# A replanned prologue order in a sliding-window attention and SwiGLU kernel

## The chip, the cores and the metric

The kernel runs on one core of a Trainium2 chip. The time is that of the device, in microseconds (us), from one launch; the kernel before has a median of 340.18 us over 11 runs (338.02 to 342.67). The engines of the core run side by side, each with its own list of instructions in order: PE (TensorE, matmuls), ACT (ScalarE), DVE (VectorE), POOL (GpSimd) and SP (SyncE). Here POOL issues the loads from memory, and SP issues copies and transposes by DMA.

## What is computed

The reference is causal attention with a window of 64 keys, and a SwiGLU layer on its output:

```python
# q, k, v: (8, 8, 576, 64) = batch, heads, positions, head size; float32
scores = q @ k.T / 8                                  # per batch and head
mask = (rel >= 0) & (rel < 64)                        # rel = query - key position
attn = softmax(where(mask, scores, -1e9))
x = (attn @ v) with heads side by side                # (4608, 512)
g = x @ w_gate                                        # (4608, 1536)
out = (g * sigmoid(g) * (x @ w_val)) @ w_out          # (4608, 512), float32
```

## The kernel before

The 4608 tokens (8 batches one behind the other) are cut into 36 chunks of 128 tokens for the attention, and into 9 groups of 512 tokens, four chunks each, for the SwiGLU layer. The 1536 hidden features are 12 blocks of 128. All matmuls are in bf16, and the loads cast on the way.

A chunk `n` goes through these steps, each a method of `_Kernel`; in the plan's entries the letter stands first and the chunk behind it:

- `ld` (`load`, line 328): POOL issues the DMA of q, k or v of the chunk into a ring of buffers, 4 for q, 4 for k (chunk modulo 4) and 10 for v. A load waits until the buffer's last reader is done. A third number is a gate: the load waits for the scores `S` of that chunk. Chunks 4, 13 and others that cross a batch's end come in two DMAs. The first two chunks of q and k are different: `first_loads` brings them as float32 by SP and ACT into the space of hT1, and `first_cast` casts them.
- `Tpe` (line 495): PE transposes q or k of a chunk, four 128x128 blocks into one PSUM bank, and ACT or DVE copies it into qT or kT. `T` (line 384) does the same as one DMA transpose on SP's queue.
- `shift` (line 347): the v tokens of a chunk are copied to a second layout, vb, offset by 64 tokens, since each half chunk of 64 queries looks at 128 keys. ACT, DVE or SP does it.
- `S` (line 400): 16 matmuls of q and k, two exps on ACT, and the mask: either a product with 0 or 1 on DVE, or (the flag `True`) a bias of -30000 that two more 512-wide matmuls add in PSUM. It needs kT of the chunk and of the one before.
- `AV` (line 437): 16 matmuls of the exps with vb and va (a column of ones gives the sums), and on DVE a reciprocal and a product, into xb.
- `X` (line 463): xb is transposed into xT, by PE and a copy, or by a DMA transpose where the plan says `'sp'`.
- `F` (`c, f0, nf, u0, u1`, line 537): for group c, nf feature blocks from f0 and chunks u0 to u1 of the group: gate and value matmuls (four steps of 128 features each), tanh on ACT (`sig`), two DVE operations (`uu`, `hT`). A whole `F` is 512 columns wide, cut either as one block by four chunks, two by two, or four by one.
- `O` (line 559): the 12 matmuls with w_out for one chunk, a copy on ACT, and the store.
- `W` (line 369) and `load_wo` (line 375): loads of feature blocks of the gate weights ('g'), the value weights ('v') and w_out, also issued by POOL.
- `warm` (line 512): matmuls of 512 columns on zeros, whose result nobody reads. `init...`: constants, mostly memsets on DVE.

`build` (line 634) first runs through the list `PLAN` (lines 151 to 198), then through a fixed `period` for groups 2 to 8, twice per group. The list holds the prologue: all attention up to chunk 11, scores of 12 and 13, all of groups 0 and 1 as far as `F` is concerned, and the four `O` of group 0. The order of the list is the order in which every engine gets its own instructions; nothing reorders them later. `_Graph` (line 31) records what each operation reads and writes, and places semaphore waits where one engine needs another's result. Every DMA takes the next of 16 counters ("lanes") of its queue, and the 17th waits for the landing of the first.

PSUM has 8 banks. In the list before the first `F`, transposes, scores and AV take turns in seven of them; from the first `F` on, four belong to `F` and four to the rest; from the first `O` on, three to the rest and one to `O`.

Of the kernel before, what the change touches and what calls it, by code (L numbers as in the profile page):

```python
# [7 lines left out]
B, H, S, D = 8, 8, 576, 64  # L8
DM, DFF = H * D, 1536
T = B * S  # L10
# [138 lines left out]

class _Kernel:  # L150
    PLAN = [
        ('first_loads', 0), ('init_va', 3, 4), ('init_va', 0, 1), ('first_loads', 1), ('init_va', 5, 6),
        ('init_va', 1, 2), ('init_va', 2, 3), ('init_va', 7, 8), ('init',), ('init_pt', 1, 'act'),
        ('first_cast', 0, 'k', 'act'), ('init_kT',), ('init_pt', 3, 'act'), ('ld', 'k', 5), ('ld', 'q', 4),
        ('init_va', 8, 9), ('warm', 7), ('init_pt', 2, 'act'), ('ld', 'k', 2), ('init_mask',),
        ('Tpe', 0, 'k', 'dve'), ('warm', 5), ('ld', 'v', 1), ('warm', 1), ('ld', 'k', 3),
        ('first_cast', 1, 'q', 'act'), ('shift', 0, 1, 'dve'), ('Tpe', 1, 'q', 'dve'), ('warm', 2),
        ('shift', 0, 0, 'act'), ('Tpe', 5, 'k', 'dve'), ('first_cast', 1, 'k', 'act'), ('ld', 'q', 3), ('init_vb',),
        ('Tpe', 4, 'q', 'dve'), ('Tpe', 1, 'k', 'dve'), ('ld', 'q', 2), ('Tpe', 2, 'k', 'dve'),
        ('shift', 1, 0, 'dve'), ('first_cast', 0, 'q', 'act'), ('ld', 'v', 3), ('Tpe', 0, 'q', 'act'),  # L160
        ('ld', 'k', 4), ('init_pt', 0, 'dve'), ('ld', 'v', 2), ('S', 1, True, False), ('init_va', 4, 5),
        ('S', 0, True, False), ('shift', 1, 1, 'dve'), ('Tpe', 3, 'k', 'dve'), ('AV', 1), ('ld', 'k', 6),
        ('Tpe', 3, 'q', 'act'), ('ld', 'k', 7), ('AV', 0), ('ld', 'q', 7), ('Tpe', 2, 'q', 'dve'),
        ('shift', 3, 0, 'act'), ('ld', 'q', 6), ('X', 1, 'act'), ('ld', 'q', 5), ('S', 3, True, False),
        ('shift', 2, 1, 'dve'), ('ld', 'v', 4), ('shift', 2, 0, 'act'), ('Tpe', 4, 'k', 'dve'), ('X', 0, 'dve'),
        ('S', 2, True, False), ('AV', 3), ('Tpe', 6, 'k', 'dve'), ('W', 'v', 3, 4), ('S', 4, True, False), ('AV', 2),
        ('Tpe', 7, 'k', 'act'), ('Tpe', 6, 'q', 'dve'), ('Tpe', 7, 'q', 'dve'), ('W', 'g', 3, 4), ('X', 3, 'act'),
        ('W', 'g', 4, 6), ('shift', 4, 0, 'dve'), ('W', 'v', 4, 6), ('W', 'g', 10, 12), ('ld', 'v', 5),
        ('shift', 3, 1, 'act'), ('X', 2, 'dve'), ('Tpe', 5, 'q', 'dve'), ('S', 6, False, False), ('W', 'v', 10, 12),
        ('S', 7, True, False), ('AV', 4), ('W', 'g', 0, 3), ('W', 'v', 0, 3), ('F', 0, 3, 1, 0, 4), ('ld', 'q', 8),  # L170
        ('F', 0, 5, 1, 0, 4), ('F', 0, 4, 1, 0, 4), ('shift', 4, 1, 'act'), ('W', 'v', 6, 8), ('ld', 'v', 6),
        ('ld', 'k', 11), ('W', 'g', 6, 9), ('S', 5, False, False), ('F', 0, 10, 2, 2, 4), ('shift', 5, 0, 'act'),
        ('F', 0, 10, 2, 0, 2), ('X', 4, 'act'), ('ld', 'q', 9), ('AV', 5), ('shift', 5, 1, 'act'), ('W', 'v', 8, 10),
        ('ld', 'k', 10), ('init_va', 6, 7), ('F', 0, 0, 3, 1, 2), ('W', 'g', 9, 10), ('ld', 'v', 13, 7),
        ('ld', 'k', 9), ('ld', 'q', 10), ('F', 0, 1, 2, 2, 4), ('ld', 'v', 7), ('Tpe', 8, 'q', 'act'),
        ('shift', 13, 0, 'sp'), ('ld', 'k', 8), ('X', 5, 'act'), ('init_va', 9, 10), ('F', 0, 0, 3, 0, 1),
        ('T', 11, 'k'), ('F', 1, 0, 2, 0, 2), ('F', 1, 3, 4, 0, 1), ('F', 0, 6, 3, 2, 3), ('shift', 6, 0, 'act'),
        ('F', 0, 0, 1, 2, 4), ('ld', 'v', 8), ('Tpe', 10, 'k', 'act'), ('F', 0, 6, 3, 3, 4), ('ld', 'q', 11),
        ('F', 0, 6, 3, 1, 2), ('shift', 6, 1, 'act'), ('AV', 6), ('ld', 'v', 9), ('shift', 7, 0, 'act'),
        ('F', 1, 8, 4, 0, 1), ('Tpe', 9, 'q', 'act'), ('ld', 'v', 12, 6), ('F', 1, 7, 1, 0, 1), ('AV', 7),  # L180
        ('load_wo', 0, 6), ('X', 6, 'act'), ('Tpe', 10, 'q', 'act'), ('load_wo', 6, 12), ('ld', 'v', 10),
        ('T', 8, 'k'), ('F', 0, 6, 3, 0, 1), ('F', 0, 9, 1, 0, 4), ('Tpe', 11, 'q', 'act'), ('X', 7, 'dve'),
        ('Tpe', 9, 'k', 'act'), ('F', 1, 5, 2, 1, 3), ('ld', 'q', 13, 7), ('ld', 'k', 12, 7),
        ('S', 10, False, False), ('ld', 'v', 11), ('S', 8, False, False), ('F', 1, 0, 2, 2, 4),
        ('shift', 8, 1, 'dve'), ('T', 12, 'k'), ('shift', 8, 0, 'act'), ('shift', 12, 1, 'sp'), ('F', 1, 8, 4, 3, 4),
        ('shift', 9, 0, 'dve'), ('ld', 'q', 12, 7), ('shift', 7, 1, 'dve'), ('T', 13, 'q'), ('S', 9, False, False),
        ('shift', 9, 1, 'act'), ('S', 11, False, False), ('F', 1, 10, 2, 1, 3), ('O', 0, 3), ('shift', 10, 0, 'act'),
        ('AV', 8), ('shift', 11, 0, 'act'), ('shift', 10, 1, 'dve'), ('ld', 'k', 15, 11), ('F', 1, 5, 3, 3, 4),
        ('T', 15, 'k'), ('O', 0, 2), ('X', 8, 'sp'), ('AV', 9), ('ld', 'q', 15, 9), ('ld', 'k', 13, 8),
        ('F', 1, 8, 2, 1, 3), ('T', 13, 'k'), ('F', 1, 7, 1, 1, 3), ('AV', 11), ('O', 0, 1), ('T', 12, 'q'),  # L190
        ('AV', 10), ('F', 1, 3, 2, 1, 3), ('ld', 'q', 14, 9), ('S', 13, False, False), ('S', 12, False, True),
        ('X', 9, 'sp'), ('F', 1, 2, 1, 0, 4), ('F', 1, 3, 1, 3, 4), ('ld', 'k', 16, 12), ('ld', 'k', 14, 8),
        ('shift', 12, 0, 'sp'), ('ld', 'v', 14, 10), ('ld', 'k', 17, 11), ('X', 11, 'sp'), ('X', 10, 'sp'),
        ('T', 15, 'q'), ('T', 14, 'q'), ('T', 14, 'k'), ('ld', 'q', 16, 11), ('ld', 'v', 15, 9), ('ld', 'q', 17, 11),
        ('shift', 11, 1, 'dve'), ('shift', 14, 1, 'sp'), ('ld', 'v', 17, 12), ('O', 0, 0), ('shift', 14, 0, 'sp'),
        ('F', 1, 4, 1, 3, 4), ('shift', 15, 1, 'sp'), ('ld', 'v', 16, 10), ('shift', 13, 1, 'sp'),
        ('shift', 15, 0, 'sp'),
    ]

    NQ = 4  # L200
# [489 lines left out]
```

## Time and profile before

| | |
|---|---|
| median of 11 runs | 340.18 us |
| the profiled execution | 342.18 us |
| its span, first to last instruction | 340.4 us |
| PE busy in the span | 326.6 us (96%) |
| DVE, ACT, POOL busy | 220.5, 145.3, 108.4 us |
| first `F` on PE begins | 23.67 us |
| first `O` on PE begins | 68.58 us |
| first period begins (its first `F`) | 89.68 us |
| clock granted to PE, mean of the span | 0.995 |

The slice rows cut the span into 40 equal parts of 8.5 us; a digit is the busy share in tenths. In a row of waits stand the waiting engine and line, who ended the wait, the sum, the number and the longest. In a row of the timeline stand the start, the time to the end, engine, line, operation and count; the end of a matmul is modelled, so that a group overlaps the next by some 0.17 us, and what counts is the distance from start to start. In a row of stretches stand the limits, their length, the busy time of PE with the number of instructions, the granted clock, the busy share of the DMA engines and GB/s. In a row of DMA issues stand the count, the size of one, and the median time from issue to landing.

The DMA slices of the prologue are full:

```profile
DMA  9999999997999999979899969696973202101022
GB/s 161 155 161 188 181 163 155 141 157 158 158 155 138 191 173 111 175 114 173 114 173 113 168 105 173 113 169 134 149 131 80 62 33 62 40 24 63 0 91 97
```

### The profile page before, as it was taken

The page shows a single profiled execution, that of the slowest core. Times are in us where ns is not written, and L with a number is a line of the kernel's source. Part 1 is how long each engine was busy: PE and PEld are TensorE (multiplying, and loading weights), DVE is VectorE, ACT ScalarE, POOL GpSimd, SP SyncE. Part 2 cuts the span into 40 slices and gives each one's busy share as a digit, 9 for nine tenths or more (in the row PEclk, how much of TensorE's full clock was granted, in tenths as well). Part 3 has the DMA queues.
Part 4 walks back from the last instruction along what each step waited for, and adds up shares of the span by engine and source line. Part 5 has one row for each costly group of instructions (what it writes and reads, how often), then busy time and mean ns, then how long its engine had stood idle before and what let it go on. Part 6 is the DMA issues. An engine that isn't in the chain of part 4 may idle for free.

```text
span 340.4 us, 7150 instructions
## 1 busy us (share of the span) xinstructions
PE 326.6 (96%) x2869; PEld 181.2 (53%) x2903; DVE 220.5 (65%) x477; ACT 145.3 (43%) x258; POOL 108.4 (32%) x135
## 2 busy tenths in 40 slices
PE   6988998999999999999999999999999999999996
PEld 2665997767544445444444444545454545444444
DVE  4786888677793939393939393939394948283610
ACT  5885566553443425252525243434343433223221
POOL 8999911430841423423232325141400000000000
PEclk9999999799999999999999999999999999999999
DMA  9999999997999999979899969696973202101022
GB/s 161 155 161 188 181 163 155 141 157 158 158 155 138 191 173 111 175 114 173 114 173 113 168 105 173 113 169 134 149 131 80 62 33 62 40 24 63 0 91 97
DMA packets 171969, 43.39 MB, mean 127 GB/s; under 512 B 158048, under 2 KB 167456, under 8 KB 171936
## 3 DMA queue, kind: packets, MB, share of 16 engines
q0 software_dynamic: 116256, 18.36, 82.2%
q1 hardware_dynamic: 48416, 14.74, 27.2%
q10 hardware_dynamic: 7264, 9.83, 8.8%
q8 instruction: 23, 0.38, 0.5%
q14 instruction: 10, 0.08, 0.1%
HBM read 37.75 MB, written 9.44 MB: 139 GB/s over the span
## 4 chain that ended last, share of the span: by engine, by line
PE 56%; DVE 19%; DMA 9%; POOL 6%; ACT 4%; issue 3%; ACTq 1%
PE ps L569 27%; PE ps L530 26%; DVE uu L551 8%; DVE hT L553 6%; DMA kn<-in_k_dram 4%; DVE xb L460 3%; DMA kT<-kn 3%; ACT ost L574 2%; DMA hT<-in_q_dram 2%; ACT sig L546 2%; POOL qn L345 2%; POOL Wg L373 1%; POOL va L345 1%; DVE rc L457 1%; POOL Wv L373 1%
## 5 line engine op out<-in xcount | busy, mean ns | idle before, releaser
L551 DVE SCALAR_TENSOR_TENSOR uu<-sig,ps 128x512 bf16<-128x512 bf16 (+3 forms) x113 | 74.6, 660 | 87.3 <-ACT sig L546 86.0
L530 PE MATMUL ps<-xT,Wv 128*128 128x512 bf16 (+2 forms) x579 | 112.7, 327 | 0.4 <-DMA Wv<-in_moe_w_val_dram 0.3
L530 PE MATMUL ps<-xT,Wg 128*128 128x512 bf16 (+2 forms) x554 | 107.3, 324 | 4.2 <-DVE uu L551 1.4
L546 ACT ACTIVATE sig<-ps 128x512 bf16<-128x512 f32 (+3 forms) x113 | 65.6, 582 | 87.4 <-PE ps L530 86.7
L569 PE MATMUL ps<-Wo,hT 128*128 128x512 bf16 x413 | 95.0, 379 | 0.4
L553 DVE SCALAR_TENSOR_TENSOR hT<-uu,ps 128x512 bf16<-128x512 bf16 (+3 forms) x113 | 75.0, 663 | 4.4 <-PE ps L530 0.5
L530 PEld LDWEIGHTS ps<-xT,Wv 128*128 128x128 bf16 x580 | 51.6, 99 | 43.9 <-issue 0.8
L345 POOL DMA_DIRECT2D kn<-in_k_dram x38 | 33.3, 881 | 124.4 <-PE ps L420 116.6
L530 PEld LDWEIGHTS ps<-xT,Wg 128*128 128x128 bf16 x580 | 48.5, 99 | 36.8 <-issue 1.9
L569 PEld LDWEIGHTS ps<-Wo,hT 128*128 128x128 bf16 x420 | 41.0, 98 | 48.6
L574 ACT ACTIVATE ost<-ps 128x512 f32<-128x512 f32 x35 | 20.9, 597 | 84.5 <-PE ps L569 84.5
L433 ACT ACTIVATE pt<-ps 128x512 bf16<-128x512 f32 x72 | 37.5, 599 | 10.0 <-PE ps L420 10.0
L345 POOL DMA_DIRECT2D va<-in_v_dram x40 | 36.3, 927 | 0.8 <-POOLq L675 0.8
L345 POOL DMA_DIRECT2D qn<-in_q_dram x38 | 33.5, 888 | 8.1 <-PE ps L530 8.1
L460 DVE TENSOR_TENSOR xb<-ps,rc 128x256 bf16<-128x256 f32 x72 | 30.6, 425 | 2.5
L435 DVE TENSOR_TENSOR pt<-pt,mask 128x512 bf16<-128x512 bf16 x60 | 23.6, 422 | 2.8 <-ACT pt L433 1.7
L451 PE MATMUL ps<-va,pt 128*128 128x65 bf16 x288 | 22.5, 193 | 0.0
L450 PE MATMUL ps<-vb,pt 128*128 128x65 bf16 x288 | 22.4, 193 | 0.0
L450 PEld LDWEIGHTS ps<-vb,pt 128*128 128x128 bf16 x288 | 20.0, 98 | 3.5
L451 PEld LDWEIGHTS ps<-va,pt 128*128 128x128 bf16 x288 | 18.9, 97 | 3.2
L420 PEld LDWEIGHTS ps<-qT,kT 64*128 64x128 bf16 x576 | 9.8, 95 | 10.7 <-issue 7.8
L420 PE MATMUL ps<-qT,kT 64*128 64x64 bf16 x576 | 12.6, 191 | 2.3 <-DMA kT<-kn 1.8
(47 smaller groups left out, 101.5 us busy)
## 6 DMA issues: line engine op xcount, KB each, us to landing
out_dram<-ost ACTq DMA_DIRECT2D x35, 256.0 KB, 4.0
va<-in_v_dram POOLq DMA_DIRECT2D x32, 128.0 KB, 7.4
kn<-in_k_dram POOLq DMA_DIRECT2D x30, 128.0 KB, 5.7
qn<-in_q_dram POOLq DMA_DIRECT2D x30, 128.0 KB, 6.4
vb<-va SPq DMA_DIRECT2D x47, 80.0 KB, 4.5
Wo<-in_moe_w_out_dram POOLq DMA_DIRECT2D x2, 768.0 KB, 21.3
Wv<-in_moe_w_val_dram POOLq DMA_DIRECT2D x4, 256.0 KB, 9.9
Wg<-in_moe_w_gate_dram POOLq DMA_DIRECT2D x2, 384.0 KB, 11.0
```

The costliest lines, as they stand in the source:

```text
L345: self.g.op("pool", lambda e, d=d, a=a: e.dma_start(d, a), reads=gate, writes=ks, dma=True)
L433: g.op("act", lambda e, po=po, p=p: e.activation(po, sv[p], ACTF.Exp, scale=SCALE), reads=[bx[p][1]], writes=[pk])
L435: g.op("dve", lambda e, po=po: e.tensor_tensor(po, po, m, ALU.mult), reads=[pk, "mask"], writes=[pk])
L450: e.matmul(av[:, j, :], pt[:, h, 0:128], vb[:, h, 0:65], start=True, stop=False)
L451: r = e.matmul(av[:, j, :], pt[:, h, 64:192], va[:, h, 0:65], start=False, stop=True)
L460: g.op("dve", lambda e, xo=xo, av=av, rb=rb: e.tensor_tensor(xo, av[:, :, 0:64], rb, ALU.mult), reads=[bk, ("rc", ir)], writes=[("xb", ix, ...
L530: r = e.matmul(bank[:, w * j:w * j + w], W[:, kk, f * 128:f * 128 + 128], xT[:, kk, 128 * u0:128 * u1], start=(kk == 0), stop=(kk == NK - 1))
L546: g.op("act", lambda e: e.activation(sig[:, 0:n], G[:, 0:n], ACTF.Tanh, scale=0.5), reads=[gk], writes=[("sig", i)])
L551: g.op("dve", lambda e: e.scalar_tensor_tensor(uu[:, 0:n], sig[:, 0:n], 1.0, G[:, 0:n], ALU.add, ALU.mult), reads=[("sig", i), gk], writes ...
L553: g.op("dve", lambda e: e.scalar_tensor_tensor(d, r3(uu[:, 0:n]), 0.5, r3(V[:, 0:n]), ALU.mult, ALU.mult), reads=[("uu", i), vk], writes=[ ...
L569: r = e.matmul(OB[:, :], hT[:, f, 128 * u:128 * u + 128], self.Wo[:, f, :], start=(f == 0), stop=(f == NF - 1))
L574: g.op("act", lambda e: e.activation(ost[:, :], OB[:, :], ACTF.Copy), reads=[ok], writes=[("ost", io)])
```

## The change

Only the list `PLAN` is different, so all steps keep their code, and the periods behind the list stay as they are. The list holds the same chunks, weights and `F` features, in a new order. What differs beyond order:

- 9 `warm` matmuls in place of 15.
- Loads: after v0 come q2, v1, k2, q3, v2, k3, v3, q4, k4, k5, v4, q5, then the first weights (blocks 0 to 2, v5, then 6 to 8); before, k5 and q4 were first, and k and q of chunks 6 and 7 also went ahead of the first weights (block 3).
- `T` of k in chunks 8 and 11 is now `Tpe` with a copy on ACT; `X` of chunks 8, 10 and 11 is now on PE with a copy on ACT instead of a DMA transpose on SP. Eight `T` and one `X` of the list are left on SP, ten and four before.
- `S` of chunk 7 has its mask on DVE instead of the bias.
- The first `F` is feature block 0 of group 0, behind `S` of chunk 5; before, it was block 3, behind `S` of 6 and 7.
- The four `O` of group 0 come in the order 1, 2, 0, 3 (before 3, 2, 1, 0), the last of them at the list's end.

The old list, cut to some of its rows, and the new one in full:

```diff
 class _Kernel:
     PLAN = [
-        ('first_loads', 0), ('init_va', 3, 4), ('init_va', 0, 1), ('first_loads', 1), ('init_va', 5, 6),
-        ('init_va', 1, 2), ('init_va', 2, 3), ('init_va', 7, 8), ('init',), ('init_pt', 1, 'act'),
-        ('first_cast', 0, 'k', 'act'), ('init_kT',), ('init_pt', 3, 'act'), ('ld', 'k', 5), ('ld', 'q', 4),
-        ('init_va', 8, 9), ('warm', 7), ('init_pt', 2, 'act'), ('ld', 'k', 2), ('init_mask',),
-        ('Tpe', 0, 'k', 'dve'), ('warm', 5), ('ld', 'v', 1), ('warm', 1), ('ld', 'k', 3),
-        ('first_cast', 1, 'q', 'act'), ('shift', 0, 1, 'dve'), ('Tpe', 1, 'q', 'dve'), ('warm', 2),
-        ('shift', 0, 0, 'act'), ('Tpe', 5, 'k', 'dve'), ('first_cast', 1, 'k', 'act'), ('ld', 'q', 3), ('init_vb',),
-        ('Tpe', 4, 'q', 'dve'), ('Tpe', 1, 'k', 'dve'), ('ld', 'q', 2), ('Tpe', 2, 'k', 'dve'),
...
-        ('S', 2, True, False), ('AV', 3), ('Tpe', 6, 'k', 'dve'), ('W', 'v', 3, 4), ('S', 4, True, False), ('AV', 2),
-        ('Tpe', 7, 'k', 'act'), ('Tpe', 6, 'q', 'dve'), ('Tpe', 7, 'q', 'dve'), ('W', 'g', 3, 4), ('X', 3, 'act'),
-        ('W', 'g', 4, 6), ('shift', 4, 0, 'dve'), ('W', 'v', 4, 6), ('W', 'g', 10, 12), ('ld', 'v', 5),
-        ('shift', 3, 1, 'act'), ('X', 2, 'dve'), ('Tpe', 5, 'q', 'dve'), ('S', 6, False, False), ('W', 'v', 10, 12),
-        ('S', 7, True, False), ('AV', 4), ('W', 'g', 0, 3), ('W', 'v', 0, 3), ('F', 0, 3, 1, 0, 4), ('ld', 'q', 8),
...
-        ('shift', 13, 0, 'sp'), ('ld', 'k', 8), ('X', 5, 'act'), ('init_va', 9, 10), ('F', 0, 0, 3, 0, 1),
-        ('T', 11, 'k'), ('F', 1, 0, 2, 0, 2), ('F', 1, 3, 4, 0, 1), ('F', 0, 6, 3, 2, 3), ('shift', 6, 0, 'act'),
...
-        ('F', 1, 8, 4, 0, 1), ('Tpe', 9, 'q', 'act'), ('ld', 'v', 12, 6), ('F', 1, 7, 1, 0, 1), ('AV', 7),
-        ('load_wo', 0, 6), ('X', 6, 'act'), ('Tpe', 10, 'q', 'act'), ('load_wo', 6, 12), ('ld', 'v', 10),
-        ('T', 8, 'k'), ('F', 0, 6, 3, 0, 1), ('F', 0, 9, 1, 0, 4), ('Tpe', 11, 'q', 'act'), ('X', 7, 'dve'),
-        ('Tpe', 9, 'k', 'act'), ('F', 1, 5, 2, 1, 3), ('ld', 'q', 13, 7), ('ld', 'k', 12, 7),
-        ('S', 10, False, False), ('ld', 'v', 11), ('S', 8, False, False), ('F', 1, 0, 2, 2, 4),
-        ('shift', 8, 1, 'dve'), ('T', 12, 'k'), ('shift', 8, 0, 'act'), ('shift', 12, 1, 'sp'), ('F', 1, 8, 4, 3, 4),
...
-        ('T', 15, 'k'), ('O', 0, 2), ('X', 8, 'sp'), ('AV', 9), ('ld', 'q', 15, 9), ('ld', 'k', 13, 8),
...
-        ('AV', 10), ('F', 1, 3, 2, 1, 3), ('ld', 'q', 14, 9), ('S', 13, False, False), ('S', 12, False, True),
-        ('X', 9, 'sp'), ('F', 1, 2, 1, 0, 4), ('F', 1, 3, 1, 3, 4), ('ld', 'k', 16, 12), ('ld', 'k', 14, 8),
-        ('shift', 12, 0, 'sp'), ('ld', 'v', 14, 10), ('ld', 'k', 17, 11), ('X', 11, 'sp'), ('X', 10, 'sp'),
...
+        ('first_loads', 0), ('init',), ('first_loads', 1), ('ld', 'q', 2), ('init_pt', 0, 'dve'),
+        ('init_pt', 3, 'act'), ('init_vb',), ('init_kT',), ('ld', 'v', 1), ('warm', 2), ('init_va', 9, 10),
+        ('init_pt', 2, 'dve'), ('init_va', 4, 5), ('init_mask',), ('warm', 7), ('init_va', 6, 7),
+        ('init_pt', 1, 'dve'), ('ld', 'k', 2), ('init_va', 8, 9), ('first_cast', 0, 'q', 'act'), ('ld', 'q', 3),
+        ('first_cast', 0, 'k', 'dve'), ('Tpe', 0, 'k', 'act'), ('init_va', 1, 2), ('ld', 'v', 2), ('ld', 'k', 3),
+        ('init_va', 0, 1), ('first_cast', 1, 'k', 'act'), ('ld', 'v', 3), ('init_va', 2, 3), ('init_va', 5, 6),
+        ('Tpe', 0, 'q', 'dve'), ('shift', 0, 0, 'act'), ('ld', 'q', 4), ('ld', 'k', 4),
+        ('first_cast', 1, 'q', 'dve'), ('shift', 0, 1, 'dve'), ('Tpe', 1, 'k', 'dve'), ('ld', 'k', 5),
+        ('S', 0, True, False), ('shift', 1, 1, 'act'), ('Tpe', 1, 'q', 'dve'), ('Tpe', 2, 'q', 'act'),
+        ('shift', 1, 0, 'dve'), ('init_va', 7, 8), ('AV', 0), ('S', 1, True, False), ('shift', 2, 0, 'act'),
+        ('Tpe', 2, 'k', 'dve'), ('Tpe', 3, 'q', 'act'), ('ld', 'v', 4), ('ld', 'q', 5), ('W', 'g', 0, 1),
+        ('init_va', 3, 4), ('shift', 2, 1, 'dve'), ('AV', 1), ('S', 2, True, False), ('Tpe', 3, 'k', 'dve'),
+        ('X', 0, 'dve'), ('X', 1, 'dve'), ('shift', 3, 1, 'act'), ('shift', 3, 0, 'dve'), ('S', 3, True, False),
+        ('Tpe', 4, 'q', 'dve'), ('AV', 2), ('W', 'v', 0, 2), ('Tpe', 4, 'k', 'act'), ('AV', 3), ('W', 'g', 1, 3),
+        ('Tpe', 5, 'k', 'act'), ('shift', 4, 0, 'dve'), ('S', 4, True, False), ('W', 'v', 2, 3), ('ld', 'v', 5),
+        ('W', 'v', 6, 7), ('X', 2, 'act'), ('W', 'g', 6, 7), ('Tpe', 5, 'q', 'dve'), ('X', 3, 'dve'),
+        ('W', 'g', 7, 9), ('AV', 4), ('W', 'v', 7, 8), ('S', 5, False, False), ('F', 0, 0, 1, 0, 4), ('ld', 'k', 6),
+        ('shift', 4, 1, 'act'), ('W', 'v', 8, 9), ('ld', 'q', 7), ('shift', 5, 0, 'dve'), ('X', 4, 'act'),
+        ('F', 0, 2, 1, 0, 4), ('ld', 'v', 6), ('F', 0, 1, 1, 0, 4), ('AV', 5), ('shift', 5, 1, 'act'),
+        ('F', 0, 6, 1, 0, 4), ('F', 0, 7, 1, 0, 4), ('X', 5, 'act'), ('F', 0, 8, 1, 0, 4), ('shift', 6, 0, 'act'),
+        ('shift', 6, 1, 'act'), ('ld', 'q', 6), ('ld', 'k', 7), ('W', 'g', 3, 6), ('F', 1, 7, 2, 0, 2),
+        ('Tpe', 7, 'k', 'act'), ('W', 'v', 3, 6), ('ld', 'k', 9), ('Tpe', 7, 'q', 'dve'), ('ld', 'v', 7),
+        ('Tpe', 6, 'q', 'dve'), ('Tpe', 6, 'k', 'act'), ('F', 1, 0, 2, 0, 2), ('ld', 'k', 8), ('S', 7, False, False),
+        ('S', 6, False, False), ('ld', 'k', 11), ('ld', 'q', 9), ('F', 1, 2, 4, 1, 2), ('F', 0, 3, 2, 0, 2),
+        ('ld', 'v', 9), ('W', 'g', 9, 12), ('Tpe', 9, 'k', 'act'), ('AV', 6), ('shift', 7, 0, 'act'), ('ld', 'v', 8),
+        ('W', 'v', 9, 12), ('Tpe', 8, 'k', 'act'), ('F', 0, 3, 2, 2, 4), ('Tpe', 11, 'k', 'act'),
+        ('F', 0, 5, 1, 0, 4), ('AV', 7), ('ld', 'q', 8), ('X', 6, 'act'), ('ld', 'q', 10), ('Tpe', 9, 'q', 'act'),
+        ('ld', 'q', 13, 7), ('ld', 'q', 11), ('ld', 'k', 10), ('F', 1, 2, 4, 0, 1), ('F', 0, 10, 2, 1, 3),
+        ('Tpe', 8, 'q', 'act'), ('F', 0, 9, 3, 3, 4), ('shift', 8, 0, 'act'), ('Tpe', 10, 'q', 'dve'),
+        ('F', 0, 9, 1, 1, 3), ('X', 7, 'act'), ('F', 0, 9, 3, 0, 1), ('Tpe', 11, 'q', 'act'), ('load_wo', 0, 6),
+        ('Tpe', 10, 'k', 'dve'), ('F', 1, 2, 2, 2, 4), ('S', 9, False, False), ('S', 8, False, False),
+        ('F', 1, 5, 2, 2, 4), ('shift', 9, 1, 'dve'), ('F', 1, 10, 1, 0, 4), ('ld', 'v', 11), ('ld', 'v', 10),
+        ('shift', 9, 0, 'act'), ('shift', 7, 1, 'dve'), ('shift', 8, 1, 'act'), ('S', 11, False, False),
+        ('load_wo', 6, 12), ('ld', 'q', 15, 9), ('shift', 10, 0, 'act'), ('ld', 'k', 13, 7), ('shift', 10, 1, 'act'),
+        ('ld', 'v', 13, 8), ('S', 10, False, False), ('F', 1, 0, 2, 2, 4), ('F', 1, 11, 1, 0, 4), ('O', 0, 1),
+        ('AV', 9), ('ld', 'v', 12, 8), ('ld', 'q', 12, 6), ('ld', 'k', 15, 10), ('F', 1, 7, 3, 2, 3), ('O', 0, 2),
+        ('ld', 'q', 14, 9), ('shift', 12, 1, 'sp'), ('shift', 11, 0, 'act'), ('AV', 8), ('ld', 'v', 16, 10),
+        ('T', 12, 'q'), ('F', 1, 4, 1, 2, 4), ('ld', 'k', 14, 9), ('T', 13, 'k'), ('shift', 13, 0, 'sp'), ('AV', 10),
+        ('shift', 12, 0, 'sp'), ('ld', 'k', 12, 6), ('X', 8, 'act'), ('T', 12, 'k'), ('O', 0, 0),
+        ('ld', 'k', 16, 10), ('ld', 'v', 15, 9), ('AV', 11), ('T', 13, 'q'), ('X', 9, 'sp'), ('X', 10, 'act'),
+        ('F', 1, 7, 3, 3, 4), ('X', 11, 'act'), ('F', 1, 9, 1, 0, 2), ('ld', 'v', 14, 9), ('ld', 'q', 17, 11),
+        ('S', 12, False, True), ('T', 15, 'k'), ('T', 14, 'k'), ('T', 14, 'q'), ('ld', 'v', 17, 12), ('T', 15, 'q'),
+        ('S', 13, False, False), ('shift', 15, 1, 'sp'), ('F', 1, 6, 1, 0, 2), ('shift', 15, 0, 'sp'),
+        ('ld', 'k', 17, 11), ('shift', 13, 1, 'sp'), ('shift', 11, 1, 'act'), ('ld', 'q', 16, 12),
+        ('shift', 14, 1, 'sp'), ('shift', 14, 0, 'sp'), ('O', 0, 3),
     ]
```

## Prediction

> **What bounds the kernel now.** I read the slices first, then TensorE's waits, then the stretches around its one long wait.
>
> ```profile
> PE   6988998999999999999999999999999999999996
> ...
> PEclk9999999799999999999999999999999999999999
> ```
>
> PE is at 9 or more in nearly every slice, so only what PE does not need, or does at a lower clock, can be saved. That lies in the prologue: until the first period of the loop (89.68 us, its first `F`) PE is busy 81.79 us and idle 7.89; afterwards 244.76 of 250.72. Nothing behind 89.68 us is edited, so the question is when that first period starts.
>
> ```profile
> PE ps L517 <- DVE wz L282: 2.1, 1, 2.1
> PE ps L420 <- DMA kT<-kn: 1.8, 1, 1.8
> ...
> PE ps L530 <- DMA Wg<-in_moe_w_gate_dram: 1.3, 1, 1.3
> ...
> PE ps L530 <- DMA Wv<-in_moe_w_val_dram: 0.3, 1, 0.3
> ```
>
> After the start, the largest wait is for a K transposed by DMA, the next for the first weights. The first one costs twice (timeline, then stretches with PE busy and granted clock):
>
> ```profile
> 58.18 0.41 PE L420 MATMUL ps<-qT,kT 64*128 64x64 bf16 x16
> 60.39 0.41 PE L420 MATMUL ps<-qT,kT 64*128 64x64 bf16 x16 [1.80 <-DMA kT<-kn]
> 60.73 1.46 PE L530 MATMUL ps<-xT,Wg 128*128 128x256 bf16 x8
> 61.99 1.91 PE L530 MATMUL ps<-xT,Wv 128*128 128x256 bf16 x8
> ```
> ```profile
> 23.15:26.57 3.42, 1.90 (x15) 1.00 1.32 163
> ...
> 57.29:60.70 3.41, 1.60 (x41) 1.00 1.28 191
> 60.70:64.10 3.40, 3.40 (x27) 0.58 1.90 172
> ```
>
> S(10) finishes, S(8) waits 1.80 us for its K, and then the clock is about half for 3.4 us: the work from 60.73 to 66.03 takes 5.30 us where the same shapes elsewhere take 3.53 (0.87+0.87 for eight 128x256 pairs, 0.89+0.90 for sixteen 128x128 ones). That is 1.77 more, 3.57 in all.
>
> **Rule against row.** The Trainium skill ("TensorE: Matmul & The Clock Gate", Why this matters for your kernels) says that idle gaps up to about 3 us keep the clock. By it the removed stall is worth 1.80. The row shows a drop after 1.80: what tells is how much of a 3.41 us stretch PE was busy, 1.60 (47%) before the drop, 1.90 (56%) without one. I use the row: 3.57.
>
> **The change, part by part.** Durations of before, start to start: a `Tpe` or `X` on PE 0.22; `S` with bias 0.86, without 0.34; `AV` 0.48; a whole `F` 1.73; `O` 2.59. On ACT a PSUM copy 0.60, a vb copy 0.73, two exps 1.08.
>
> *Order of loads.* POOL issues a q/k/v load every 0.87 us, and their landings are 0.86 apart: k5 8.79, then q4 9.68 up to q5 21.01 and v4 21.89, fifteen tensors. After, chunks 6 and 7 no longer go ahead of the weights, so q5 is the 12th tensor after v0 and lands at 8.8+11x0.86 = 18.3; Wg block 0 then at 18.9, Wv 0-1 about 20.9, Wg 1-2 22.8, Wv 2 23.7. (A block takes 0.65 us in the long run; the first multi-block ones landed 1.5 late before, 26.49 after 23.32, and I carry that.)
>
> *First F.* Before: 23.67, with 16 Tpe and 7 S done. After: 12 Tpe, 6 S, 5 AV, 4 X, 10.6 us of PE work, so PE isn't the limit; ACT is. Its list from the exps of S(0) to the copy of X(2): 5x1.08 + 3x0.73 + 5x0.60 = 10.6 us. S(0) can end at 8.8 (k of chunk 1 lands 6.96, cast 0.63, Tpe, S), so ACT ends at 19.4; S(4) comes late by some 0.4 (k5 16.5, transposed and copied). First F: 19.8 to 20.2.
>
> *Fewer warm matmuls*, 9 for 15. They end near 5.2 either way, where they wait for the casts, so nothing is gained; the warm-up rule of the same page is kept (about 3.9 us). But in the stretch 6.09 to 9.50 PE now has only a Tpe, S(0) and two Tpe, about 1.5 to 1.6 us, where it was busy 2.53. The nearest row is the 1.60 followed by half clock. Bounds: 0 to 1.7 us. I take 0.7, since ACT paces the next 3.4 us: first F at 20.9. Wg 1-2 (22.8) and Wv 2 are then on time (F(0,0) and X(4) end at 22.85); without this loss they would cost 0.65 in its place.
>
> *What is behind the first F.* Before: 89.68-23.67 = 66.01, less waits 1.27+0.31+1.80 and 1.77 of clock = 60.86. After comes more: 4 Tpe (0.88) and one S (0.34) move behind it, T(8,k), T(11,k), X(8), X(10), X(11) turn from DMA into PE work, 5x0.22 = 1.10. Their copies, 0.60 on ACT or 0.42 on DVE, lie beside F's (ACT 5.4 of 8.5 us in 51 to 59.5). Sum 63.2. First period: 20.9+63.2 = 84.1, **5.6 earlier**; I keep 5.5, leaving 0.1 for the second copy's queue.
>
> *SP's and POOL's queues.* With T(11,k), T(8,k) gone, the K ring no longer waits for DMA transposes (POOL k <- DMA kT 7.5 us), and S(8) to S(11) wait for copies alone. What is late next: q13 goes into the buffer of q9 and POOL stands until Tpe(9,q), about 46.4; q11, k10, both Wo, v11, v10 are queued behind. Landings follow: q11 51.9, k10 52.8, Wo 0-5 56.7, Wo 6-11 62.3. PE needs q11 at 54.1, k10 at 54.5, the Wo at 64.7: 1.7 to 2.4 us in hand, cost 0. Then k15 waits for S(10), and q14, v16, k14, k12 behind it: four issues 3.5, k12's landing 6.5 (the row of 60.55), T(12,k) 5.8 = 15.8 us; T(13,q) follows 1.3 later. Between S(10) and S(12) PE has 18.3 us of work. Cover 2.5 us (1.5 for S(13)), cost 0.
>
> **Sum.** The profiled execution took 342.18 (span 340.4, 1.8 around it): 336.7 after. It is 2.0 above the median of 340.18, and the runs lie in two groups, 338.0 to 340.2 and 341.6 to 342.7. If a median run has the stall and the half clock too, it goes to 334.7; if it has not the half clock, the gain is 3.7 and it goes to 336.5. **I forecast 336.5.**
>
> **Rivals.** (1) *The walk holds*, at most one short wait new: 58%, 334 to 338.4. (2) *New small losses eat most of it*: the first weights 1.5 late, or the q13 stop pushes Wo beyond the 2.4 us in hand, with one or two new stretches at half clock (1.7 each). For it: before had such a wait on Wg, and both covers are short; against: four loads fewer stand ahead of the weights. 336.5+1.5+1.7 = 339.7, at the edge of no change: 24%. (3) *Slower: S(12) waits for its K.* The chain k15 to T(12,k) is all in series. The rows for a load and a transpose in a full DMA queue are 12.6 and 11.0 instead of 6.5 and 5.8:
>
> ```profile
> kn<-in_k_dram POOLq DMA_DIRECT2D x4, 128.0 KB, 12.6
> ...
> kT<-kn SPq DMA_TRANSPOSE x2, 11.0
> ```
>
> Then 3.5+12.6+11.0 = 27.1 against 18.3: 8.8 of stall and 1.8 of half clock, 336.5+10.6 = 347. It decides from a chain of about 22 us (18.3+5.5-1.8) on. Against it: the queue at that point holds about seven loads, not sixteen, and Wo has landed; in 66 to 90 us K and Q transposes took 4.4 and 5.8. 13%. (4) *It doesn't do what it says*: T or the copies just shift the same wait to ACT's queue (Tpe(8,k) and Tpe(11,k) are copied by ACT behind sig and exp), no gain: 340, 5%.
>
> **Numbers.** About 0.5% (1.7 us) is what can be told from no change. Faster: nearly all of (1), a part of (2), 0.64; within: most of (2) and (4), 0.21; slower 0.15. The range 333.5 to 341.0 reaches below to both bounds at their good end (no start loss, median with stall) and above over (2) and (4); most of (3) is left out.
>
> **What would show it.** Right: no wait of PE for kT before the first O, no clock below 1.0 from 20 to 80 us, first F at 20 to 21.5, first O at 64 to 66, first period at about 84. Wrong: PE waiting on k10, q11 or Wo (POOL's stop), on kT at S(12) (rival 3), or sig and exp on ACT running late behind the new copies.

## The result, and the profile after

The changed kernel has a median of 336.39 us over 12 runs (334.97 to 337.35). The kernel before, run beside it and in the earlier comparison, now has 340.59 us over 47 runs (336.78 to 344.31). The comparison puts the ratio at 0.9901, with a 95% interval of 0.9873 to 0.9929: about 1% faster, and the forecast was 336.5. (The comparison leaves disturbed runs out, so this isn't quite the quotient of the two medians, 0.988.) The spread shrank too: 2.4 us after, 7.5 us before.

The profiled execution after is its quickest run, 334.97 us. Its page, the line of busy times and the slices:

```profile
PE 323.6 (97%) x2783; PEld 176.4 (53%) x2819; DVE 220.4 (66%) x475; ACT 147.8 (44%) x261; POOL 109.3 (33%) x136
...
PE   6999999999999999999999999999999999999996
...
DMA  9999999999999999999999989797943111101022
GB/s 164 155 180 174 174 130 157 175 189 140 168 166 214 134 159 116 163 117 178 112 167 127 166 113 180 105 161 126 180 99 89 33 63 32 65 0 64 2 95 94
```

The two slices at 8 in PE's row of before are gone, and so is the PEclk row; the granted clock of this execution is 1.000. PE is busy 3.0 us less (323.6 against 326.6), mostly the half clock and the warm matmuls; the rest of the 7.3 us by which the span is shorter is idle time. The DMA engines are as full as before through the prologue; only the order of what they carry is different. (Both traces lack some 35 of PE's records, so its busy times are a little low and its idle times a little high.) The list of PE's waits:

```profile
PE ps L529 <- DVE uu L550: 1.4, 9, 0.2
PE ps L516 <- DVE wz L281: 1.3, 1, 1.3
PE ps L502 <- ACT kn L276: 1.1, 1, 1.1
PE ps L502 <- ACT qn L276: 0.3, 1, 0.3
PE ps L502 <- DMA kn<-in_k_dram: 0.3, 1, 0.3
```

All of these stand at the start (L516 is the first warm matmul, L502 a transpose), or are the 0.2 us of the loop that were there before; these stand at groups of three 512-wide matmuls where the others have four, and the trace of the kernel with late q13 (below), which lacks no record, has none of them, so they are lost records and not waits. No wait for kT, Wg or Wv is in it. The timeline at the four places that the prediction named: the first `F`, the `S` pair of chunks 9 and 8, the first `O`, and the first `F` of the loop:

```profile
20.33 0.81 PE L529 MATMUL ps<-xT,Wg 128*128 128x512 bf16 x3 [0.16 <-DVE rc L456]
...
55.88 0.64 PE L419 MATMUL ps<-qT,kT 64*128 64x64 bf16 x32
...
64.09 2.75 PE L568 MATMUL ps<-Wo,hT 128*128 128x512 bf16 x12
...
83.05 1.03 PE L529 MATMUL ps<-xT,Wg 128*128 128x512 bf16 x4
```

`S` of 9 and 8 stand as one group of 32 matmuls without a gap; before, `S(8)` stood alone behind 1.80 us of waiting. The first period begins at 83.05, 6.63 us earlier than in the profiled execution of before. The table splits that at the first `F`, for the traces that are compared below; the last column is the execution's time less the begin of the first period.

| kernel, time of its profiled execution | first `F` | from there to the first period | first period | the rest |
|---|---|---|---|---|
| before, 342.18 | 23.67 | 66.01 | 89.68 | 252.5 |
| before again 1, 343.11 | 24.01 | 67.13 | 91.14 | 252.0 |
| before again 2, 339.25 | 24.89 | 62.24 | 87.13 | 252.1 |
| after, 334.97 | 20.33 | 62.72 | 83.05 | 251.9 |
| after again, 336.63 | 20.94 | 62.62 | 83.56 | 253.1 |
| before with K transposes on PE, 340.59 | 24.24 | 62.98 | 87.22 | 253.4 |
| after with late q13, 335.36 | 20.41 | 63.06 | 83.47 | 251.9 |
| after with K transposes by DMA, 337.08 | 19.99 | 65.18 | 85.17 | 251.9 |
| after with late weights, 340.33 | 23.06 | 64.86 | 87.92 | 252.4 |
| new order with DMA transposes, 342.85 | 20.05 | 68.70 | 88.75 | 254.1 |

Two things can be read here. The rest is about 252 us for every kernel, plus what the first period still loses (a wait of 1.4 us in the row of 340.59 and of 1.0 in after again, half clock in the last row). And the first `F` is what sets the three traces of before and the two of after apart always, by 2.7 to 4.6 us; the stretch behind it sets them apart only in the executions of before in which the clock dropped.

### The profile page after: what moved, and what is told of

Same layout as the page of the kernel before. It is cut to its first block, busy times and chain, and to the rows that moved or that the text cites. A ratio compares the mean times of both kernels' runs of the same rounds, so it can differ in the third digit from the quotient of the medians.

```text
span 333.1 us, 6973 instructions
## 1 busy us (share of the span) xinstructions
PE 323.6 (97%) x2783; PEld 176.4 (53%) x2819; DVE 220.4 (66%) x475; ACT 147.8 (44%) x261; POOL 109.3 (33%) x136
## 3 DMA queue, kind: packets, MB, share of 16 engines
q0 software_dynamic: 116784, 18.36, 79.6%
## 4 chain that ended last, share of the span: by engine, by line
PE 70%; DVE 18%; ACT 3%; POOL 3%; issue 2%; DMA 2%; ACTq 1%; POOLq 0%
PE ps L529 37%; PE ps L568 27%; DVE uu L550 7%; DVE hT L552 6%; DVE xb L459 3%; DMA kn<-in_k_dram 2%; ACT sig L545 2%; ACT ost L573 2%; DVE rc L456 1%; PE ps L419 1%; POOL va L344 1%; PE ps L502 1%; PE ps L450 1%; POOL qn L344 1%; PE ps L449 1%
## 5 line engine op out<-in xcount | busy, mean ns | idle before, releaser
L550 DVE SCALAR_TENSOR_TENSOR uu<-sig,ps 128x512 bf16<-128x512 bf16 (+2 forms) x111 | 74.4, 670 | 83.5 <-ACT sig L545 82.4
L529 PE MATMUL ps<-xT,Wv 128*128 128x512 bf16 (+2 forms) x530 | 111.3, 339 | 0.1
L529 PE MATMUL ps<-xT,Wg 128*128 128x512 bf16 (+2 forms) x505 | 106.0, 337 | 2.6 <-DVE uu L550 1.4
L545 ACT ACTIVATE sig<-ps 128x512 bf16<-128x512 f32 (+2 forms) x111 | 65.3, 589 | 80.3 <-PE ps L529 80.1
L552 DVE SCALAR_TENSOR_TENSOR hT<-uu,ps 128x512 bf16<-128x512 bf16 (+2 forms) x111 | 74.6, 672 | 3.8
L529 PEld LDWEIGHTS ps<-xT,Wv 128*128 128x128 bf16 x532 | 48.9, 98 | 45.0 <-DMA Wv<-in_moe_w_val_dram 0.5
L529 PEld LDWEIGHTS ps<-xT,Wg 128*128 128x128 bf16 x532 | 45.4, 98 | 35.9
L573 ACT ACTIVATE ost<-ps 128x512 f32<-128x512 f32 x35 | 20.9, 597 | 81.7 <-PE ps L568 81.7
L344 POOL DMA_DIRECT2D va<-in_v_dram x40 | 35.1, 886 | 0.8 <-DVE wz L281 0.8
L434 DVE TENSOR_TENSOR pt<-pt,mask 128x512 bf16<-128x512 bf16 x62 | 24.5, 423 | 2.6 <-ACT pt L432 1.1
L449 PE MATMUL ps<-vb,pt 128*128 128x65 bf16 x288 | 22.8, 193 | 0.5 <-ACT pt L432 0.2
L450 PE MATMUL ps<-va,pt 128*128 128x65 bf16 x288 | 22.8, 193 | 0.0
L456 DVE RECIPROCAL rc<-ps 128x4 f32<-128x4 f32 x72 | 12.5, 173 | 2.1 <-PE ps L450 2.1
```

The lines of the kernel that those rows point to most:

```text
L344: self.g.op("pool", lambda e, d=d, a=a: e.dma_start(d, a), reads=gate, writes=ks, dma=True)
L434: g.op("dve", lambda e, po=po: e.tensor_tensor(po, po, m, ALU.mult), reads=[pk, "mask"], writes=[pk])
L449: e.matmul(av[:, j, :], pt[:, h, 0:128], vb[:, h, 0:65], start=True, stop=False)
L450: r = e.matmul(av[:, j, :], pt[:, h, 64:192], va[:, h, 0:65], start=False, stop=True)
L529: r = e.matmul(bank[:, w * j:w * j + w], W[:, kk, f * 128:f * 128 + 128], xT[:, kk, 128 * u0:128 * u1], start=(kk == 0), stop=(kk == NK - 1))
L545: g.op("act", lambda e: e.activation(sig[:, 0:n], G[:, 0:n], ACTF.Tanh, scale=0.5), reads=[gk], writes=[("sig", i)])
```

## The experiments

**Before and after once more.** Three executions profiled anew, with no edit: is the stall of before, with its half clock, in every execution?

> The kernel before once more, unchanged, for a second trace. Theory (its times spread from 337 to 344 because S(8) waits for a DMA transpose in a full queue, sometimes long enough to halve the clock, sometimes not): the time goes with the wait for kT before 62 us and the half clock behind it; an execution of about 338 has a wait under 1 us and no half clock, one of 343 more than the 3.57 us of the first trace. Rival (the spread comes from the loop or from the start): waits before 62 us within 0.5 us of the first trace whatever the time.

> The kernel before a third time, unchanged, with the same expectations as for the second trace.

> The kernel after once more, unchanged. Its first trace was its fastest run, 334.97. Theory (POOL's stop for q13 costs some runs a wait of PE on Wo, q11 or k10, which is why the kernel with q13 behind Wo is at 335.26 and steadier): at a time of about 336.4 a wait of 0.5 to 1.5 us on one of these between 50 and 66 us. Rival (the difference lies elsewhere): a wait of this size before 50 us, on weights or at the start, or none.

The timeline of the first, and then its clock in the slices:

```profile
60.78 0.61 PE L420 MATMUL ps<-qT,kT 64*128 64x64 bf16 x16 [3.15 <-DMA kT<-kn]
61.32 1.89 PE L530 MATMUL ps<-xT,Wg 128*128 128x256 bf16 x8
```
```profile
PEclk9999999599999999999999999999999999999999
```

And the timeline of the second:

```profile
59.50 0.41 PE L420 MATMUL ps<-qT,kT 64*128 64x64 bf16 x16 [1.52 <-DMA kT<-kn]
59.84 1.05 PE L530 MATMUL ps<-xT,Wg 128*128 128x256 bf16 x8
```

The same `S(8)` waited 1.52, 1.80 and 3.15 us in three executions. Eight 128x256 matmuls behind it took 1.05 us after the shortest wait and 1.89 after the longest: none, one and two stretches of 3.41 us at half clock followed. So the stall is in all three traces, but the clock's part of it isn't, and an execution with a wait of 1.5 us, not under 1 us, is what a time of 339 means. The runs without a trace say the same by their mean granted clock. Of the 63 runs of before beside the experiments, 26 have a clock of 0.995 or less and a median of 342.39 (341.9 without the ten slowest), 37 have full clock and 339.35; they overlap only between 340.6 and 341.3. All 12 runs of after have 0.999 or more. The mean tells that the clock dropped somewhere in the run, not that it was behind `S(8)`.

After, looked at again, took 336.63. No wait on loads showed between 50 and 66 us, where I had expected one. Its 1.7 us over the first trace are at other places: 0.6 before the first `F`, where this time the clock was half from 8.58 to 12.00 us, and a wait in the first period:

```profile
91.54 0.41 PE L419 MATMUL ps<-qT,kT 64*128 64x64 bf16 x16
92.95 0.41 PE L419 MATMUL ps<-qT,kT 64*128 64x64 bf16 x16 [0.99 <-DVE uu L550]
```

The view names DVE, which had long been done. The DMA transpose of q of chunk 15 landed at 92.86, and the `S` that reads it starts 0.09 later: that is the releaser. In the first trace it landed at 91.20, in time.

**Only the K transposes of chunks 8 and 11,** made in the kernel before. Here and below, rows of the list are cut to the entries that differ.

```diff
-        ('T', 11, 'k'),
+        ('Tpe', 11, 'k', 'act'),
...
-        ('T', 8, 'k'),
+        ('Tpe', 8, 'k', 'act'),
```

> The kernel before with only the two K transposes of chunks 8 and 11 turned from DMA into PE transposes with a copy on ACT. Theory (each part pays by itself): PE's 1.80 us wait at S(8) and the 1.77 us of half clock behind it go, 0.44 us of PE work comes: 3.1 us less than the profiled 342.18, that is 1.3 to 3.1 us less than the median of before (ratio 0.991 to 0.996), the first period at about 86.5 instead of 89.68, no clock below 1.0 between 57 and 67 us. Rival (the order of loads does it all, a wait elsewhere takes the place of this one): ratio 0.998 to 1.002, and a new wait of over 1 us on PE between 50 and 70 us.

340.02 us (339.54 to 341.42), ratio 1.0003 [0.9974, 1.0032]: nothing. Yet the edit did what it was meant to do. The stretch from the first `F` to the first period fell from 66.01 to 62.98, there was no wait at `S(8)`, and none of 12 runs has a clock below 0.999. What was won was lost again in the first period:

```profile
PE ps L420 <- DMA kT<-kn: 1.4, 1, 1.4
...
96.66 0.64 PE L420 MATMUL ps<-qT,kT 64*128 64x64 bf16 x32 [1.39 <-DMA kT<-kn]
```

This is `S` of 14. In before its k was transposed at 96.75 and needed at 97.65, so that the late period hid it. With the period 2.5 us earlier the chain stays where it was: on POOL the load of k14 stands behind the load of k16, which waits for `S(12)`; k14 was issued at 83.26, landed at 89.10, and was transposed at 96.61. Against the full-clock runs of before (339.35) the edit alone costs 0.7, against the others (342.39) it gains 2.4.

**The same, and k14 ahead of k16.** If POOL's order makes that wait, a swap takes it away.

```diff
-        ('ld', 'k', 16, 12), ('ld', 'k', 14, 8),
+        ('ld', 'k', 14, 8), ('ld', 'k', 16, 12),
```

> The kernel before with the two K transposes on PE, as in the first experiment, and one swap more: the load of k14 stands ahead of that of k16, which waits for S(12). Theory (what the two PE transposes saved, 2.46 us at the first period, was handed back in the first period, where S(14) waited 1.39 us for K of chunk 14 by a chain S(12), load k16, load k14, transpose): with k14 no longer behind that gate the wait goes and the time is 1.2 to 1.6 below the first experiment's 340.0, 338.4 to 338.9, no PE wait for kT between 87 and 100 us. Rival (the transposes save nothing in most runs, the wait in the first period is chance): 339.6 to 340.4.

339.04 (338.78 to 340.04), ratio 0.9982 [0.9951, 1.0013], 1.0 below the kernel without the swap, and the kT wait is gone from the trace. The cause of the wait is shown. How much the two edits bring is not: by the ratios 0.18% of the 0.99%, with an interval from nothing to half, and before itself had 340.08 beside this kernel and 340.59 beside the one without the swap.

**After, without the K transposes on PE** (chunks 8 and 11 by DMA again; this and the edits below are made in the kernel after).

```diff
-        ('Tpe', 8, 'k', 'act'), ('F', 0, 3, 2, 2, 4), ('Tpe', 11, 'k', 'act'),
+        ('T', 8, 'k'), ('F', 0, 3, 2, 2, 4), ('T', 11, 'k'),
```

> The kernel after with K of chunks 8 and 11 transposed by DMA again. Theory (what hurt was the place, a transpose issued late into a queue full with Wo): here the transposes are issued at about 39 to 40 us, behind some eight loads, land by about 50, and S(9) at 56 needs them, so there is no wait, and PE has 0.44 us less to do: 336.4 minus 0.4, within 335.5 to 337. Rival (DMA transposes among loads cost by themselves, slowing the load stream): the loads behind them land 3 to 5 us later, Wo at 67 instead of 64, the first O waits, and the time is 338.5 to 341.

336.40 (336.11 to 337.08), ratio 0.9875 [0.9820, 0.9929]: as after. No wait for kT came back. In the new order the two transposes are issued at 39.2 and 40.95, some 15 us ahead of their `S`, so by the median the edit that the prediction priced highest isn't needed in this order. Its trace, of the slowest of its six runs, isn't free of waits, though: 0.36 us at 49.56 and 0.61 ahead of the first `O`, as in the kernel with both edits below, and one at a place where its list is still that of after:

```profile
23.31 1.04 PE L529 MATMUL ps<-xT,Wg 128*128 128x512 bf16 x4 [1.20 <-DMA Wg<-in_moe_w_gate_dram]
```

The gate weights of blocks 1 and 2 landed at 23.26 here and at 22.11 in the trace of after. That is the first term of the prediction's second rival, and it can befall after too.

**The weights behind chunks 6 and 7 again.** The four loads are taken out where they stood; the rest of the new list stays.

```diff
-        ('ld', 'v', 4), ('ld', 'q', 5), ('W', 'g', 0, 1),
+        ('ld', 'v', 4), ('ld', 'q', 5), ('ld', 'k', 6), ('ld', 'q', 7), ('ld', 'q', 6),
...
+        ('ld', 'k', 7), ('W', 'g', 0, 1),
```

> The kernel after with k and q of chunks 6 and 7 loaded ahead of the first weights, as before. Four loads at 0.86 us put every early weight 3.4 us later: Wg 0 at 22.5, Wv 0 to 1 at 24.2, Wv 2 at 26.6. Theory (the first F is what the load order buys): the first F waits about 2.2 us, the next about 1.5, the first period starts 3 to 3.5 us later than 83.05, and a stretch of half clock may add 1.7: 339.5 to 341.5. Rival (only the transposes mattered, the early weights are made up for later by waits that are there anyway): 336 to 337.5.

340.90 (338.91 to 342.78), ratio 1.0017 [0.9980, 1.0053]: the whole gain is gone. The timeline at the first `F`:

```profile
20.30 0.41 PE L419 MATMUL ps<-qT,kT 64*128 64x64 bf16 x16
23.06 1.02 PE L529 MATMUL ps<-xT,Wg 128*128 128x512 bf16 x4 [2.36 <-DMA Wg<-in_moe_w_gate_dram]
24.39 1.86 PE L529 MATMUL ps<-xT,Wv 128*128 128x512 bf16 x4 [0.30 <-DMA Wv<-in_moe_w_val_dram]
```

PE is ready within 0.4 us of after, waits for weights that come four loads later, and four matmuls take 1.86 us in place of 1.03: half clock again, from 24.42 to 27.83. Eleven of the 12 runs have a clock of 0.995 or less; the one with full clock took 338.91. So of the 4.5 us, by that one run, some 2.5 are the wait itself and the rest mostly the clock. Not all of that is behind this wait: the trace also has half clock from 7.35 to 10.77, before the weights are needed.

**The new order without fewer DMA transposes.** The K transposes as in the experiment above, and `X` of 8, 10 and 11 by DMA too.

```diff
-        ('X', 8, 'act'),
+        ('X', 8, 'sp'),
...
-        ('X', 10, 'act'),
+        ('X', 10, 'sp'),
...
-        ('X', 11, 'act'),
+        ('X', 11, 'sp'),
```

> The kernel after with all five transposes given back to DMA (K of chunks 8 and 11, X of 8, 10 and 11): the new order alone. Theory (the order of loads is the gain, DMA transposes cost nothing where they are not awaited): 335.5 to 337, as after. Rival (fewer transposes by DMA matter, those of X at the end of the list most, since their landing at 79 to 84 us is what the first period waits for): 1 to 3 us more, 337.5 to 339.5, with a PE wait for xT or kT.

342.26 (341.63 to 343.44), ratio 1.0068 [1.0039, 1.0097]: 5.9 above after, and slower than before. My theory is wrong here, and the rival is too small. The timeline at the first period:

```profile
81.77 2.11 PE L568 MATMUL ps<-Wo,hT 128*128 128x512 bf16 x9
88.75 1.87 PE L529 MATMUL ps<-xT,Wg 128*128 128x512 bf16 x4 [4.88 <-DMA xT<-xb]
90.42 1.84 PE L529 MATMUL ps<-xT,Wv 128*128 128x512 bf16 x4
```

The `X` of 10 and 11 are issued at 79.29 and 80.61 and take 7.6 and 8.05 us. The period could begin at about 83.7; it begins 88.75, when the last one has landed, and then runs its first 3.4 us at half clock. Before had these transposes by DMA too, and they cost nothing there: issued at 80.88 and 83.22, they had landed by 85.54, and its period began at 89.68. Not only the period is earlier. In before POOL's next loads are issued from 84.84 on, behind these transposes; in the new order from 78.12 on, and the transposes run among them. Issue to landing in before and here:

```profile
xT<-xb SPq DMA_TRANSPOSE x2, 2.3
...
xT<-xb SPq DMA_TRANSPOSE x2, 7.8
```

The kernel above with only its K transposes by DMA differs from this one by the three `X` alone, and took 336.40.

**The load of q13 behind Wo.** POOL stands from 40.9 to 46.3 us for the buffer of q13, with q11, k10 and Wo behind it:

```profile
46.30 2.26 POOL L344 DMA_DIRECT2D qn<-in_q_dram  x3 [5.40 <-PE ps L502]
```

```diff
-        ('ld', 'q', 13, 7), ('ld', 'q', 11),
+        ('ld', 'q', 11),
...
-        ('load_wo', 6, 12), ('ld', 'q', 15, 9),
+        ('load_wo', 6, 12), ('ld', 'q', 13, 7), ('ld', 'q', 15, 9),
```

> The kernel after with the load of q13 behind both halves of Wo, so that POOL does not stand from 40.9 to 46.3 us for the buffer of q9. Theory (PE never waits for what stands behind that stop): q11, k10 and Wo land some 4 us earlier and the time stays, 336.0 to 336.8. Rival (the stop costs a part of the runs a wait on Wo or k10): 0.5 to 1.5 less, 335 to 335.9.

335.26 (334.81 to 335.42), ratio 0.9858 [0.9814, 0.9903], 1.1 below the median of after and within 0.6 us over six runs. This is the quickest of all kernels tried. The intervals of the two ratios overlap; that five of its six runs are below 335.4, where one of 12 of after is, makes the gain likely all the same, if not its size: the median of before beside the kernels of this section moved by up to 0.6 us. Wo landed at 54.0 and 59.1 instead of 57.3 and 64.0. But neither trace of after shows PE stopping for these loads, so where after loses its 1.1 is not shown. (The kernel without warm matmuls, below, does stop 0.53 us for Wo ahead of its first `O`.)

**Both: q13 late, K transposes by DMA.** The two edits above together.

> The kernel after with q13 behind Wo, as in the experiment at 335.26, and the K of chunks 8 and 11 transposed by DMA again. Theory: 0.44 us of PE work less and the transposes (issued at about 39, needed at 56) still hidden: 334.7 to 335.3. Rival (with POOL no longer standing the DMA queue is full when they run, and they delay k10, q11 and Wo): 335.5 to 337.

336.50 (336.29 to 337.31), ratio 0.9894 [0.9846, 0.9942]: no run of it is as quick as the slowest of the kernel with late q13 alone. Its timeline, two places:

```profile
49.30 1.03 PE L529 MATMUL ps<-xT,Wv 128*128 128x256 bf16 x8 [0.86 <-DMA Wv<-in_moe_w_val_dram]
...
65.66 2.76 PE L568 MATMUL ps<-Wo,hT 128*128 128x512 bf16 x12 [0.61 <-ACT pt L432]
```

| median, us | K transposes by DMA | on PE |
|---|---|---|
| q13 early | 336.40 | 336.39 |
| q13 late | 336.50 | 335.26 |

These are medians of different sets of runs, good to some half a microsecond. By them, each edit is worth about 1.1 to 1.2 only where the other is made too; the ratios (0.9875 and 0.9901 above, 0.9894 and 0.9858 below) have overlapping intervals, so this is likely and not shown. With the transposes in the queue, weights come late around 49 us and `S`'s exps ahead of the first `O`; that POOL's stop is what is left without them is a reading, not a measurement.

**The warm matmuls.** Fifteen of them again, and none.

```diff
-('warm', 7)
+('warm', 13)
```

> The kernel after with 15 warm matmuls instead of 9. Theory (the casts and the loads pace the start): they end at about 7.2 instead of 5.0 and push Tpe(0,k) and Tpe(0,q) from 4.9 and 5.5 to about 7.3, S(0) from 7.28 to about 8.0 and, through ACT, the first F by 0.4 to 0.7: 336.7 to 337.2. Rival (the six matmuls kept the clock up): 1 to 2 us less than after in runs in which the clock dropped, 335 to 336.

335.91 (335.60 to 338.39), ratio 0.9878 [0.9824, 0.9932]: no difference from after that can be told.

```diff
-('warm', 2)
...
-('warm', 7)
```

> The kernel after without any warm matmul. Theory (loads and ACT pace the first 20 us, PE has room): the transposes and S of chunks 0 and 1 run at half clock for one or two stretches of 3.4 us, the first F comes 0 to 0.7 us later: 336.4 to 337.2. Rival (a cold PE paces the start): first F at 22 us or later, 338 or more.

337.61 (335.97 to 338.96), ratio 0.9924 [0.9885, 0.9963], 1.2 above after: between what the theory and its rival gave. Until about 10 us PE's matmuls run slow (the two 512-wide ones of the mask take 1.06 us there, 0.59 in after), though the rows of stretches show the granted clock as 1.00; the first `F` comes at 21.41 and the first period at 84.80. Nine warm matmuls are worth about 1 us, six more nothing that these runs can tell.

## Why the prediction was right, point by point

- **Order of loads, first `F`.** The step was right. q5 landed at 18.36 (worked out 18.3), Wg block 0 at 19.09 (18.9), Wv 0-1 at 20.77 (20.9), Wg 1-2 at 22.11 (22.8), Wv 2 at 23.13 (23.7). The first `F` stood at 20.33 and 20.94 in two traces. That the gain hangs on this order is shown by the late weights: without it the time is 340.90. It hangs as much on the three `X`, so the two can't be added up.
- **"PE isn't the limit; ACT is."** The time came out, the reason did not. In the first trace k5 landed at 17.02 (16.5 worked out), and PE and ACT waited for it:

```profile
17.06 0.40 PE L502 MATMUL ps<-ident,kn 128*128 128x128 bf16 x4 [0.27 <-DMA kn<-in_k_dram]
...
17.50 0.60 ACT L276 ACTIVATE kT<-ps 128x512 bf16<-128x512 bf16 x1 [0.63 <-PE ps L502]
```

From there the chain that ends at the first `F` goes over PE and then DVE's copies and products, 18.84 to 20.25; in the second trace DVE is on it from 16.54 on. ACT is on neither after 13.2. DVE has no term in the prediction's sum for the first `F`.
- **0.7 us for a clock drop at the start** was a middle between 0 and 1.7. In the first trace no 3.41 us around these have PE busy for less than 2.0, more than the 1.5 to 1.6 worked out, and no drop came; in the second PE was busy 1.67 of 5.17 to 8.58, a drop came and cost 0.6. None of the 12 timed runs has a clock below 0.999, so 0 is right for the median.
- **The K stall, 3.57 us.** Mechanism right, size wrong for the median. 1.80 and 1.77 are right for the execution that I read. But the wait is 1.5 to 3.2 us, and 37 of 63 runs have no half clock behind it. The prediction left this open, and by its two cases chose the one without half clock: a gain of 3.7 from 340.18. The runs of that kind have 339.35 and go to 336.4, a gain of 2.95. The start 0.8 too high and the gain 0.75 too large cancel, so part of the agreement is luck.
- **"Nothing behind 89.68 us is edited"** is true of the list's periods, but not of what they wait for. The loads and transposes of chunks 14 and 15 come from the prologue, and the earlier the period begins, the nearer they are: 1.39 us in the kernel with K transposes alone, 0.99 in the second trace of after, 0 in its first.
- **Five transposes turned to PE** were priced at 1.10 us of PE work, which fits: from the first `F` to the first period it took 62.72 and 62.62 us, 63.2 forecast. What was missed is what they avoid. I looked for the end of the K wait and gave the three `X` no gain; left on DMA, they cost 5.9 us in the new order, since they run among loads and land at 88.7, and a period that could begin at 83.7 waits for them.
- **POOL's stop at q13** was foreseen to 0.1 us (until 46.4, measured 46.30; q11 51.9 and 51.78; k10 52.8 and 52.74). But Wo 6-11 landed at 63.98, not 62.3, and the first `O` stood at 64.09: 0.1 us in hand in place of 2.4. The cost was 0 in the traces, with nothing to spare; this is the second term of rival 2, and the late q13 makes it likely that about 1 us was to be had.
- **Rival 3, `S(12)` waiting.** The K of 12 landed at 76.35 and `S(12)` began at 79.01: 2.7 us of cover, 2.5 forecast. The load took 6.95 us, the transpose stood 2.05 before it was issued and took 2.68, together 11.7 where 12.3 were forecast and far from the 12.6 and 11.0 of the full queue.
- **Rule against row.** The row decides. The Trainium skill ("TensorE: Matmul & The Clock Gate", Why this matters for your kernels) gives gaps of about 3 us without loss; here half clock followed waits of 1.80 and 2.36 us, and not 1.52. What parts them is the share of a 3.41 us stretch in which PE was busy. Where the granted clock falls, its edges show which stretch counts; in before it is half a microsecond later than the one that the prediction read, with the same 1.60, and the fall is a whole one:

```profile
57.81:61.22 3.41, 1.60 (x42) 1.00 1.26 191
61.22:64.63 3.41, 3.41 (x23) 0.50 2.09 166
```

The other falls followed stretches with 1.78, 1.67, 1.29, 1.06 and 0.00 us (late weights, after again, before again 1, late weights, new order with DMA transposes). No fall followed 2.07 (new order, 81.80 to 85.22), nor the wait of 1.52 in before again 2, around which every 3.41 us have 1.88 or more. So the limit lies near half a stretch. It is not sharp to a tenth: before again 1 had 1.76 in 5.14 to 8.55 (counted back from its fall) and kept its clock. By this, the prediction's row holds, and a wait well under 3 us is enough if PE has little to do around it.

What stays open is where runs of after without a trace lose up to 2.4 us over the quickest: their clock is full, so it's not the clock. A late transpose in the first period, as in the second trace, would fit, and so would gate weights that land 1.15 us later, as in the kernel with K transposes by DMA, or Wo with 0.1 us to spare; none was seen to do it in those runs. Nor were the smaller differences of the two lists tried alone: how the weight loads are cut, gates of loads, copies moved between ACT and DVE, the mask of chunk 7, the order of the four `O`.

## What to carry to other kernels

Load first what the engine that sets the end needs first; here four loads of 0.87 us ahead of the first weights were worth 4.5 us, part of it by the clock that drops behind a wait. When a stage is moved earlier, go through every transfer that its first readers need, and ask whether it was on time, or only hidden by the stage being late: that is how a kT at 96.6 us turned from free to 1.4 us. Ask also what it will run beside: an xT that took 2.3 us took 8 among the loads that had moved up with it, and cost 5.9. And where a kernel's runs scatter by 2%, look at two or three executions before a stall of one of them is taken out of the median.

## What the runs showed of the hardware

- The granted clock falls to 0.50 for a stretch of 3.41 us (before, 61.22 to 64.63) or for two (before again 1, 59.76 to 66.58). The first always followed a stretch in which PE was busy 1.78 us or less. The length of the wait alone doesn't tell: 3.15 us had two stretches of half clock, 4.88 us (new order with DMA transposes) had one. The waits of one program vary enough (1.52, 1.80, 3.15) for it to fall in some executions only; its runs with and without lie at 342.39 and 339.35. A stretch takes some 1.7 us of that (an estimate, half of 3.41); longer waits are likely the rest.
- A DMA transpose of the same tile size took 2.7 us in a quiet queue (k of 12), and 8.9 and 10.0 us among loads (q of 15, in two executions of the same kernel); one of xb 2.3 us in before and 7.6 to 8.05 among loads.
